# Scores of every chunk as plain float32 products instead of three float32r products of split q and k

## The chip, the core and the metric

The kernel runs on one core of a Trainium2 chip. The core has a matrix engine (TensorE, PE in the rows; its weight loads are PEld), a vector engine (VectorE, DVE), a scalar engine (ScalarE, ACT), a general engine (GpSimd, POOL) and a queue engine that starts transfers (SyncE, SP). Each engine works through its own list of instructions in order and waits where a semaphore says so. The metric is the device time of one execution in microseconds; several runs give a median.

## The reference

For two batches of 768 rows the reference computes an attention layer with 8 heads of 64 columns, then two feed-forward blocks. Cut to what matters here:

```python
scores = scale * np.matmul(q, k.transpose(0, 1, 3, 2))      # scale 1/8
keep = is_global | is_local                                 # first 8 keys, and the last 96
scores = np.where(keep, scores + bias, -1e9)
a = softmax(scores)
attn = np.matmul(a, v)                                      # to (2, 768, 512)
h = relu(attn @ w_in)
x = (h * sigmoid(conv3(h))) @ w_out
u, v = split(relu(x @ w_in2))
out = (u * (w_spatial @ norm(v) + b_spatial)) @ w_out2
```

Only the line with `scores` is computed in another way by the change; what is computed stays the same.

## The kernel before

The 2 x 768 rows are cut into six chunks of 256 rows (three for each batch). In a chunk there are four units, each a pair of heads, and in a unit two steps of 128 rows. So the attention has 24 units and 48 steps. A step goes through these tasks, in the order of the functions `scores`, `soften`, `halves`, `weigh` and `turn_x`:

- scores (L801): for both heads of the pair, q times 256 columns of k, into two PSUM banks. Head 0 lies in partitions 0 to 63 and head 1 in 64 to 127.
- soften: VectorE adds the bias and takes the extreme of each row (L820, tile `sb`, and `nm` beside it), for chunks 2 to 5 a fixed power is added to it (L833, tile `nb`, on GpSimd or VectorE), and ScalarE takes the exponential (L838).
- halves: for chunks 0 and 1 (`PLAINS`) TensorE turns the result (L851); for chunks 2 to 5 it is split into two float16 parts, `ph` (a cast, L474 on ScalarE or L478 on VectorE, and a subtraction, L488 on GpSimd or VectorE), which a transfer turns into `pt`.
- weigh: products with v (L906 plain, L912 to L914 in float16 parts), then VectorE divides (L918, L922, L923, tile `xk`).
- turn_x: TensorE turns `xk` (L954), and it is split into float16 parts `x`.

The same engines also do the first feed-forward block (L1028 products with w1, L1041 to L1066 the convolution and the gate, the parts `hh` and `hl`, L1098 products with w2) beside the attention, decode the float64 weights into float16 parts (L655 to L670 on ScalarE and VectorE, a cast, and a subtraction on GpSimd), and afterwards do the second block (L1173, L1246, L1278, L1308).

How the scores are made depends on the chunk. `NATS` lists the chunks whose q and k go into the products as they were loaded, and `qk_load` makes no parts of them. For the others ScalarE casts the whole tile of q and k (672 columns) to float32r (`qh`), and GpSimd or VectorE subtracts it from the tile, which leaves the low part in place (`qk` as float32r). The lines of `scores` that choose:

```python
if u // NPAIR in NATS:
    pairs = [(self.m("qk", u), self.m("qk", u))]
    cost, reads = 0.79, [("qk", u)]
else:
    hi, lo = self.m("qh", u, dt=F32R), self.m("qk", u, dt=F32R)
    pairs = [(hi, hi), (lo, hi), (hi, lo)]
    cost, reads = 0.57, [("qk", u), ("qh", u)]
```

The order on each engine isn't the order of the source. A planner (`Plan`) collects tasks with a cost for each engine that may do them, works out in six rounds which engine takes which task and when, and writes the instructions in that order; the lists are then fixed. A task's cost, the 0.79 and 0.57 above among them, so decides also where other tasks stand and on which of two engines a cast or subtraction runs. Until a planned time of 70 us the planner fills planned gaps of TensorE with products that nobody reads (L999).

Of the kernel before, what the change touches and what calls it, by code (L numbers as in the profile page):

```python
# [40 lines left out]

LEAD_TICKS, LEAD_STEPS = 12, 8

NATS, PLAINS = (0, 1, 2), (0, 1)

BIASES = 2

# [1535 lines left out]
```

## Time and profile before

| what | us |
|---|---|
| median of 3 runs | 381.29 (381.17 to 382.48) |
| the profiled execution, whole | 380.87 |
| its span, first to last instruction | 379.2 |
| TensorE busy | 360.5 |
| VectorE, ScalarE, GpSimd busy | 271.5, 265.4, 156.3 |

The span is what the engines' instructions cover; 1.67 us of the execution lie around it. TensorE's busy time overstates its work, since the ends of its pipelined products overlap: the distance from one start to the next is the better measure of what a product costs. The kernel has a first part to about 77 us, in which weights are decoded beside the attention of chunks 0 to 2; a middle part to about 245 us, with the attention of chunks 3 to 5 (scores from 90 to 187 us) and the rest of the first block; and a last part that is products almost alone.

### The profile page before, as it was taken

What the parts mean: (1) busy time and instruction counts of PE and PEld (TensorE: products, weight loads), DVE (VectorE), ACT (ScalarE), POOL (GpSimd) and SP (SyncE); (2) the same over time, 40 slices, a digit from 0 to 9 for tenths busy, and PEclk for the clock granted to TensorE, in tenths of its full rate; (3) what the DMA queues carried; (4) which work ended last, traced back from release to release, by engine and by line L of the source; (5) the groups of instructions that cost most, each with busy time, mean ns of one, the idle gap of its engine ahead of it and who ended that gap; (6) DMA issues with size and microseconds to landing.
All of it is one profiled execution on the core that took longest, in us unless ns stands there. A gap on an engine that the chain in (4) does not pass through costs nothing.

```text
span 379.2 us, 7892 instructions
## 1 busy us (share of the span) xinstructions
PE 360.5 (95%) x2893; PEld 254.7 (67%) x2893; DVE 271.5 (72%) x695; ACT 265.4 (70%) x650; POOL 156.3 (41%) x221
## 2 busy tenths in 40 slices
PE   8989889788999999999999999999999999999995
PEld 5767767557877888888779766676456565555543
DVE  5899999977985798799896498678568355151610
ACT  5977999678997798799898467676976434232332
POOL 5253447866486578578664034142125200000000
PEclk9987999989999999999999999999999999999999
DMA  7979422567639534974669000005510000202022
GB/s 223 406 253 309 166 94 73 111 186 176 171 95 267 108 83 94 204 186 119 83 99 346 1 2 0 2 2 159 169 62 0 0 2 0 86 0 85 0 85 91
DMA packets 46254, 43.60 MB, mean 115 GB/s; under 512 B 34816, under 2 KB 36608, under 8 KB 45696
## 3 DMA queue, kind: packets, MB, share of 16 engines
q1 hardware_dynamic: 46208, 43.03, 39.9%
q8 instruction: 24, 0.39, 0.4%
q14 instruction: 22, 0.18, 0.1%
HBM read 31.48 MB, written 3.15 MB: 91 GB/s over the span
## 4 chain that ended last, share of the span: by engine, by line
PE 51%; DVE 25%; ACT 11%; issue 6%; POOL 3%; DMA 2%; DVEq 0%; POOLq 0%; ACTq 0%
PE bank L1278 12%; PE bank L1308 8%; PE bank L1246 8%; PE bank L1098 6%; DVE wk_dt_float L665 5%; PE bank L1173 5%; DVE bank L1041 5%; DVE wk_dt_float L670 4%; DVE sb_dt_float L820 3%; PE bank L801 3%; PE bank L1028 3%; DVE wk_dt_float L662 3%; DMA pt_dt_float<-ph_dt_float 2%; ACT sb_dt_float L838 2%; PE bank L999 1%
## 5 line engine op out<-in xcount | busy, mean ns | idle before, releaser
L1028 PE MATMUL bank<-x_dt_float,w1h_dt_float 128*128 128x260 f16 (+1 forms) x384 | 65.1, 273 | 0.5 <-ACT pt_dt_float L474 0.4
L1098 PE MATMUL bank<-hl_dt_float,w2h_dt_float 128*128 128x254 f16 (+2 forms) x192 | 52.9, 275 | 1.4 <-POOL hl_dt_float L488 1.3
L1098 PE MATMUL bank<-hh_dt_float,w2l_dt_float 128*128 128x254 f16 (+2 forms) x192 | 52.9, 276 | 0.3 <-POOL w2l_dt_float L488 0.3
L1098 PE MATMUL bank<-hh_dt_float,w2h_dt_float 128*128 128x254 f16 (+2 forms) x192 | 53.0, 276 | 0.0
L1028 PE MATMUL bank<-x_dt_float,w1l_dt_float 128*128 128x260 f16 (+1 forms) x192 | 52.3, 273 | 0.0
L1041 DVE SCALAR_TENSOR_TENSOR bank<-hp_dt_float,cwt,bank 128x254 f32<-128x254 f32 (+2 forms) x96 | 46.0, 484 | 5.9 <-ACT bank L1035 3.4
L1278 PE MATMUL bank<-ws_dt_float,vn_dt_float 128*128 128x384 f16 x288 | 47.3, 326 | 0.0
L488 POOL TENSOR_TENSOR hl_dt_float<-ac_dt_float,hh_dt_float 128x256 f16<-128x256 f32 (+2 forms) x44 | 32.6, 747 | 33.5 <-ACT hh_dt_float L474 28.8
L488 POOL TENSOR_TENSOR ph_dt_float<-sb_dt_float,ph_dt_float 128x512 f16<-128x512 f32 x29 | 36.6, 1264 | 18.7 <-ACT ph_dt_float L474 16.7
L1028 PEld LDWEIGHTS <-w1h_dt_float 128*128 128x128 f16 x384 | 36.7, 97 | 7.3 <-issue 1.8
L1098 PEld LDWEIGHTS <-w2h_dt_float 128*128 128x128 f16 x384 | 36.8, 99 | 6.7 <-ACT sb_dt_float L838 0.3
L1278 PEld LDWEIGHTS <-vn_dt_float 128*128 128x128 f16 x288 | 28.2, 98 | 18.8
L820 DVE CUSTOM_DVE_ANT_0 sb_dt_float<-bank,bias_dt_float 128x256 f32<-128x256 f32 (+1 forms) x96 | 35.0, 400 | 5.4 <-PE bank L801 3.1
L838 ACT ACTIVATE sb_dt_float<-sb_dt_float,nb_dt_float 128x256 f32<-128x256 f32 (+1 forms) x64 | 30.0, 496 | 8.0 <-POOL nb_dt_float L833 5.6
L474 ACT CAST g_dt_float<-bank 128x384 f16<-128x384 f32 x16 | 7.7, 479 | 33.8 <-DVE bank L1285 33.8
L1246 PE MATMUL bank<-ys_dt_float,w3uh_dt_float 128*128 128x384 f16 x128 | 31.2, 326 | 0.0
L1282 DVE SCALAR_TENSOR_TENSOR bank<-bank,bb_dt_float 128x384 f32<-128x384 f32 x16 | 9.1, 566 | 29.4 <-PE bank L1278 29.4
L1308 PE MATMUL bank<-w4h_dt_float,g_dt_float 128*128 128x512 f16 (+1 forms) x104 | 28.9, 363 | 0.0
L1173 PE MATMUL bank<-w3vh_dt_float,ys_dt_float 128*128 128x512 f16 x96 | 28.5, 379 | 0.0
L1308 PEld LDWEIGHTS <-g_dt_float 128*128 128x128 f16 x156 | 15.2, 98 | 15.6
L665 DVE SCALAR_TENSOR_TENSOR wk_dt_float<-raw_dt_float,wk_dt_float 128x512 int32<-128x512 int32 x28 | 24.9, 896 | 0.2
L662 DVE TENSOR_SCALAR wk_dt_float<-wk_dt_float 128x512 int32<-128x512 int32 x28 | 18.6, 673 | 8.5 <-ACT wk_dt_float L655 8.4
(157 smaller groups left out, 890.8 us busy)
## 6 DMA issues: line engine op xcount, KB each, us to landing
raw_dt_float<-in_w SPq DMA_DIRECT2D x20, 512.0 KB, 5.1
qk_dt_float<-in_qk SPq DMA_DIRECT2D x24, 336.0 KB, 3.9
v_dt_float<-in_vb SPq DMA_DIRECT2D x4, 1024.0 KB, 6.0
out_x<-wk_dt_float SPq DMA_DIRECT2D x11, 256.0 KB, 2.0
raw_dt_float<-in_wst SPq DMA_DIRECT2D x6, 384.0 KB, 4.7
raw_dt_float<-in_w3v SPq DMA_DIRECT2D x4, 512.0 KB, 6.4
raw_dt_float<-in_w3u SPq DMA_DIRECT2D x4, 512.0 KB, 6.2
v_dt_float<-in_vb SPq DMA_DIRECT2D x2, 768.0 KB, 6.1
```

Source lines behind the costliest of these rows:

```text
L488: self.engines[e].tensor_tensor(out=out, in0=in0, in1=in1, op=ALU.subtract)
L662: nc.vector.tensor_scalar(out=fi, in0=fi, scalar1=3, scalar2=None, op0=ALU.logical_shift_left)
L665: nc.vector.scalar_tensor_tensor(out=fi, in0=lo, scalar=29, in1=fi, op0=ALU.logical_shift_right, op1=ALU.bitwise_or)
L820: nc.vector.tensor_tensor_reduce(out=sb[:, h, :n], in0=self.ps(self.sp[s][h])[:, :n], in1=self.m("bias", 2 * p + h)[:, t0 : t0 + n], scale ...
L838: nc.scalar.activation(out=sb[:, h, :n], in_=sb[:, h, :n], func=AF.Exp, scale=-1.0, bias=nb[:, h : h + 1])
L1028: nc.tensor.matmul(self.ps(acc)[:, :nx], w[f][:, k * P : (k + 1) * P], x[:, k, x0:], start=k == n == 0, stop=k == 3 and n == 2,)
L1041: nc.vector.scalar_tensor_tensor(out=ac(), in0=near(j), scalar=tap(j), in1=ac(), op0=ALU.mult, op1=ALU.add)
L1098: nc.tensor.matmul(ps(), w[2 * d + k // 4][:, k % 4 * P : (k % 4 + 1) * P], x, start=k == n == 0, stop=k == 7 and n == 2,)
L1173: nc.tensor.matmul(ps(), x[:, y, k, tk], w[k], start=n == 0, stop=n == 11)
L1246: nc.tensor.matmul(ps(), w[e4][:, k * P : (k + 1) * P], x[:, y, k, s], start=n == 0, stop=n == 11)
L1278: nc.tensor.matmul(ps(), v[:, k, x, ek], w[:, k, s], start=n == 0, stop=n == 17)
L1308: nc.tensor.matmul(ps(), x[:, y, k, tk], w[k][:, at], start=n == 0, stop=n == 11)
```

## The change

`NATS` now lists all six chunks:

```diff
-NATS, PLAINS = (0, 1, 2), (0, 1)
+NATS, PLAINS = (0, 1, 2, 3, 4, 5), (0, 1)
```

`PLAINS` is as before: chunks 2 to 5 keep the fixed power and the float16 parts of the probabilities. For the 12 units of chunks 3 to 5 the cast `qh` and the subtraction `qk` go, and each of their 24 steps has two float32 products (one for each head) in place of six float32r products. The planner gets other tasks and costs and so gives another order: the fill products L999 are 33 instead of 35; six `nb` additions go from VectorE to GpSimd, so do four `hl` subtractions and two `ph` subtractions, and two `ph` casts go from ScalarE to VectorE.

TensorE's list at the first step of chunk 3 (`qh` and `qk` are q and k of a unit, `xk` an attention result to be turned):

```order
-L801 MATMUL bank<-qh_dt_float32r 128x256 x2
-L801 MATMUL bank<-qh_dt_float32r,qk_dt_float32r 128x256 x2
-L801 MATMUL bank<-qk_dt_float32r,qh_dt_float32r 128x256 x2
+L801 MATMUL bank<-qk_dt_float_85 128x256 x2
```

Six products of a step are two.

VectorE's list around the division of the last unit of chunk 1 (L918 to L923; `xk` is what TensorE turns next, `wk` a weight that is being decoded, `ys` a part of the first block's result):

```order
 L665 SCALAR_TENSOR_TENSOR wk_dt_float_135<-raw_dt_float_134,wk_dt_float_135 128x512
-L670 SCALAR_TENSOR_TENSOR wk_dt_float_135<-raw_dt_float_134,wk_dt_float_135 128x512
 L484 SCALAR_TENSOR_TENSOR ys_0_dt_float_202<-bank,ys_0_dt_float_202 128x254
 L918 TENSOR_SCALAR r_dt_float_158<-bank 128x4
 L922 RECIPROCAL r_dt_float_158<-r_dt_float_158 128x4
 L923 TENSOR_TENSOR xk_dt_float_156<-bank,r_dt_float_158 128x256
+L670 SCALAR_TENSOR_TENSOR wk_dt_float_135<-raw_dt_float_134,wk_dt_float_135 128x512
```

The last step of a weight's decoding (L670) stood ahead of the division and stands behind it now.

VectorE's list some twenty instructions later, around the divisions of chunk 2's first two units:

```order
 L1041 SCALAR_TENSOR_TENSOR bank<-hp_dt_float_183,cwt,bank 128x256 x2
-L488 TENSOR_TENSOR ph_dt_float_203<-sb_dt_float_129,ph_dt_float_203 128x512
-L1066 SCALAR_TENSOR_TENSOR ac_dt_float_184<-bank,hp_dt_float_183 128x256
+L478 CAST ph_dt_float_203<-sb_dt_float_136 128x512
 L918 TENSOR_SCALAR r_dt_float_148<-bank 128x4
 L922 RECIPROCAL r_dt_float_148<-r_dt_float_148 128x4
 L923 TENSOR_TENSOR xk_dt_float_149<-bank,r_dt_float_148 128x256
```

A subtraction and a gate ahead of the division have gone, and a cast, which needs a later step's exponential, stands there now.

## Rows read from the trace of the kernel before

**Rows 1.** Page, part 1: busy us (share of the span) xinstructions.

```profile
PE 360.5 (95%) x2893; PEld 254.7 (67%) x2893; DVE 271.5 (72%) x695; ACT 265.4 (70%) x650; POOL 156.3 (41%) x221
```

**Rows 2.** Stretches: length, busy time of each engine (instructions), granted clock, DMA share, GB/s.

```profile
70.00:80.00 10.00, 6.63 (x42) 5.00 (x42) 9.26 (x21) 6.80 (x16) 7.96 (x10) 0.86 0.73 193
...
90.00:100.00 10.00, 8.72 (x104) 7.43 (x101) 9.65 (x28) 9.52 (x26) 4.88 (x9) 1.00 0.88 181
...
120.00:130.00 10.00, 10.00 (x106) 8.29 (x104) 5.68 (x20) 6.64 (x18) 4.44 (x7) 1.00 0.61 132
...
150.00:160.00 10.00, 10.00 (x118) 8.44 (x116) 7.59 (x24) 7.35 (x18) 7.05 (x10) 1.00 0.81 176
```

**Rows 3.** TensorE's waits from 85 to 245 us: total, times, longest.

```profile
PE bank L954 <- DVE xk_dt_float L923: 2.9, 3, 1.3
PE bank L1098 <- POOL hl_dt_float L488: 1.3, 2, 0.8
PE bank L912 <- DVE nm_dt_float L820: 0.5, 1, 0.5
PE bank L912 <- DMA pt_dt_float<-ph_dt_float: 0.2, 1, 0.2
```

**Rows 4.** TensorE in order of time, a float32 step: start, duration, operation.

```profile
82.49 0.70 PE L801 MATMUL bank<-qk_dt_float 64*128 64x256 f32 x4
83.12 0.28 PE L1098 MATMUL bank<-hh_dt_float,w2h_dt_float 128*128 128x254 f16 x1
```

**Rows 5.** TensorE in order of time, a float32r step and what follows it.

```profile
122.39 0.39 PE L801 MATMUL bank<-qh_dt_float32r 64*128 64x256 f32 x2
...
122.93 0.20 PE L912 MATMUL bank<-vh_dt_float,pt_dt_float 128*128 128x65 f16 x1
```

**Rows 6.** Groups by form: xcount, busy us, mean ns, idle before.

```profile
L474 ACT CAST qh_dt_float32r<-qk_dt_float 128x672 fp32r<-128x672 f32 x12 | 9.0, 753 | 0.2 <-PE bank L801 0.2
L488 POOL TENSOR_TENSOR qk_dt_float32r<-qk_dt_float,qh_dt_float32r 128x672 fp32r<-128x672 f32 x11 | 17.8, 1616 | 0.2
L488 DVE TENSOR_TENSOR qk_dt_float32r<-qk_dt_float,qh_dt_float32r 128x672 fp32r<-128x672 f32 x1 | 1.3, 1314 | 0.6 <-ACT qh_dt_float32r L474 0.6
L833 POOL TENSOR_TENSOR nb_dt_float<-nm_dt_float,shift 128x2 f32<-128x2 f32 x26 | 10.7, 413 | 4.0 <-DVE nm_dt_float L820 3.6
L478 DVE CAST vn_dt_float<-wk_dt_float 128x512 f16<-128x512 f32 x1 | 1.4, 1376 | 0.0
```

**Rows 7.** VectorE in order of time, 73 to 77 us.

```profile
74.40 1.68 DVE L670 SCALAR_TENSOR_TENSOR wk_dt_float<-raw_dt_float,wk_dt_float 128x512 int32<-128x512 int32 x1
76.00 0.41 DVE L484 SCALAR_TENSOR_TENSOR ys_dt_float<-bank,ys_dt_float 128x254 f16<-128x254 f32 x1
...
76.73 0.42 DVE L923 TENSOR_TENSOR xk_dt_float<-bank,r_dt_float 128x256 f32<-128x256 f32 x1
```

**Rows 8.** TensorE in order of time, 77 us; [idle before <-releaser].

```profile
77.21 0.69 PE L954 MATMUL bank<-ident,xk_dt_float 128*128 128x128 f32 x2 [3.37 <-DVE xk_dt_float L923]
```

**Rows 9.** Short stretches around the same wait, columns as in rows 2.

```profile
76.50:77.00 0.50, 0.00 (x0) 0.00 (x0) 0.45 (x2) 0.50 (x2) 0.19 (x1) 1.00 0.91 377
77.50:78.00 0.50, 0.50 (x4) 0.38 (x3) 0.33 (x2) 0.50 (x2) 0.50 (x2) 0.50 1.05 442
80.50:81.00 0.50, 0.50 (x4) 0.25 (x4) 0.11 (x1) 0.50 (x2) 0.00 (x0) 0.92 1.10 216
```

**Rows 10.** TensorE in order of time, waits from 90 to 117 us.

```profile
92.23 0.44 PE L954 MATMUL bank<-ident,xk_dt_float 128*128 128x128 f32 x2 [1.28 <-DVE xk_dt_float L923]
...
103.81 0.19 PE L912 MATMUL bank<-vh_dt_float,pt_dt_float 128*128 128x65 f16 x1 [0.48 <-DVE nm_dt_float L820]
...
112.11 0.27 PE L1098 MATMUL bank<-hl_dt_float,w2h_dt_float 128*128 128x256 f16 x1 [0.82 <-POOL hl_dt_float L488]
```

**Rows 11.** Chain of waits, ScalarE's pieces before that: start, us.

```profile
91.12 0.43 ACT sb_dt_float L838
91.88 0.52 ACT ph_dt_float L474
```

## The prediction

> **What bounds the kernel now.** First I read the page's busy times: TensorE 95%, VectorE 72%, ScalarE 70%, GpSimd 41% [rows 1]. The reader is to see that TensorE leads, but that a share over the whole run does not say where it waits. So next I read the stretches of 10 us [rows 2]. From 70 to 80 us TensorE is busy 6.63 of 10 us and VectorE 9.26: here VectorE, which decodes the weights, holds the end. From 90 to 100 us TensorE has 8.72 while VectorE and ScalarE have 9.65 and 9.52: TensorE is held up by engines that are nearly full. From 120 to 130 and from 150 to 160 us TensorE is busy throughout, and VectorE and ScalarE have 2.4 to 4.3 us of slack: TensorE alone is the bound. Third I read what TensorE waited for from 85 to 245 us, the part that the change touches directly [rows 3]: 2.9 us in three waits for an attention result `xk`, 1.3 us in two for `hl`, 0.5 and 0.2 us in two more before the products with v. That is 4.9 us in all, and it is the most that less work on the other engines can give back there. The helpers lose some 30 us of busy time below; almost none of it can show in the total.
>
> **The change part by part.**
>
> *Score products.* A float32 step starts at 82.49 us and the next product at 83.12: 0.63 us [rows 4]. A float32r step starts at 122.39 and the next product at 122.93: 0.54 us [rows 5]. So each of the 24 steps costs TensorE 0.09 us more, 24 x 0.09 = +2.2 us. Both rows are at the full granted clock and include the switch to what follows. I take all of it as being on the path, because TensorE has no slack in most of the stretches. If every step stood just ahead of a wait, it would cost nothing; so the term lies between 0 and +2.2.
>
> The Trainium skill ("FP8 and Floating Point Precision", section "TensorE Precision Notes") says that a true float32 product takes four passes through the array, and that the reduced form truncates float32 to what the array takes natively, which I read as one pass. By that rule alone a step would be 2 x 4 x 256 = 2048 columns against 6 x 256 = 1536, at 2.4 GHz an estimate of 0.85 against 0.64 us, and 24 steps would cost +5.1 us. The trace has less for both, 0.63 and 0.54 us; the two heads of a step use different halves of the array's rows, and their records overlap. Here the measured step decides.
>
> *Casts and subtractions that go.* ScalarE loses 12 casts of 0.753 us, 9.0 us. GpSimd loses 11 subtractions of 1.616 us, 17.8 us, and VectorE one of 1.3 us [rows 6]. None is on TensorE's path by itself: from 120 us on TensorE was busy beside all of them [rows 2]. What they may give is a part of the waits. Four of the 12 casts stand before 110 us, where ScalarE is full, so its list is some 3 us shorter when TensorE makes its waits of 1.28 us for `xk`, 0.48 us before the products with v and 0.82 us for `hl` [rows 10], 2.6 us. I take half, -1.3 us, since the float32r cast at 88 us is only one of many pieces that the chain runs through, and the exponential and cast at 91 to 92 us [rows 11] stay. Of the remaining 2.3 us (the other two waits for `xk`, the second for `hl` and the one for a transfer [rows 3]) I take a third, -0.8: TensorE is nearly full from there on, and what it waits for last is the end of the attention's own chain. Together -2.1, with ends 0 and -4.9. Six `nb` additions of 0.41 us and six more subtractions come to GpSimd, about 7 us against 17.8 that leave, so its list is shorter anyhow.
>
> *The division at 77 us.* This is no part of the edit itself; it comes from the new order. VectorE's L670 runs from 74.40 and the next instruction starts at 76.00; only then come `ys`, the division and `xk` at 76.73 [rows 7]. TensorE had been idle for 3.37 us when it turned `xk` at 77.21 [rows 8]. In the new order L670 stands behind the division, the rest of VectorE's list up to there has the same tasks in a slightly other order, and TensorE has the same products ahead of it. So `xk` is ready 1.6 us earlier: -1.6 us, ends 0 and -3.37. What is late instead is the decoded block of w2 that L670 finishes; its cast and subtraction follow up to 1.6 us later, and TensorE has two blocks of twelve products and two score steps of 0.63 us ahead of its use, which cover it.
>
> *The clock after it.* The granted clock is 1.00 in that wait, 0.50 from 77.5 to 78.0 and 0.92 from 80.5 to 81.0 [rows 9]: it fell to the 1.2 GHz level after TensorE had been idle for 3.37 us, and came back some 3.5 us later. At half speed 3.5 us do the work of 1.75. After the wait of 1.28 us at 92.23 [rows 10] the stretch of 90 to 100 us shows 1.00 throughout [rows 2]. The new wait of about 1.8 us lies between the two, nearer to the one that held, but the 10 us before it are also thinner. I take half, -0.85 us, ends 0 and -1.75.
>
> *Others.* Two fill products fewer, two casts moved to VectorE and single moves of casts behind 245 us I cost at nothing: VectorE has 2.4 to 4.3 us of slack in 10 where TensorE is full [rows 2], and TensorE's own work hides them. Where that cover is missing (80 to 100 us) they are a rival below.
>
> *Sum.* +2.2 - 2.1 - 1.6 - 0.85 = -2.35 us. The profiled execution took 380.87 us (span 379.2 and 1.67 around it), so 378.5 us. It lies 0.4 us below the median of 381.29; I leave the forecast at 378.5. The ends of all terms together would be 380.87 + 2.2 = 383.1 and, with the products at 2.2, 380.87 + 2.2 - 4.9 - 3.4 - 1.75 = 373.0.
>
> **The rivals.**
>
> *The waits stay (381.5 us).* The attention of a chunk is a long chain over all engines: scores, bias, exponential, split, a turn by transfer, products, division. If it is this chain's length and not the load of ScalarE that makes TensorE wait, nothing comes back of the 4.9 us, and the clock falls as before. Then it is +2.2 - 1.6: 381.5. For it: the waits for `xk` are waits for the last link of that chain, and one is for a transfer [rows 3]. Against: from 90 to 100 us ScalarE and VectorE are over 95% busy [rows 2], so the chain is queued and not only long.
>
> *A cast on VectorE holds the division (383.9 us, slower).* In the new order a `ph` cast stands right ahead of the division of chunk 2's first units. It needs an exponential from ScalarE, which ended at 91.55 in the trace, with the cast of the same kind following at 91.88 [rows 11], and VectorE can't pass it. If that exponential doesn't come earlier, VectorE casts from 91.6 (1.38 us by the one cast of that form on VectorE [rows 6]), divides in about 0.75 us, and TensorE turns `xk` at about 93.8 to 94.6 in place of 92.23, a loss of up to 2.4 us. Then 380.87 + 2.2 + 2.4 - 1.6 = 383.9. It decides if ScalarE reaches this exponential less than 2 us sooner than before. For it: one more link between two full engines. Against: a subtraction on VectorE and a gate stood in the same place before, and ScalarE has lost two float32r casts and two `ph` casts ahead of it, some 2.7 us.
>
> *Float32 products at the price of four passes (381.4 us).* If products beside other work, not the few steps at 82 us, show the real price, the sum has 2.9 us more: 378.5 + 2.9. This is the skill's rule above as a rival. Against: the step at 82.49 us stands between blocks of other products, as the new ones will, and has 0.63 us [rows 4].
>
> **How the numbers follow.** The forecast has 0.50, with a range of its own of 376.0 to 379.6: the clock wholly kept or lost (0.85 either way), the waits given back by half more or less. The waits stay has 0.27, the cast on VectorE 0.18, four passes 0.05. A measurement of this kernel tells about 0.5% (1.9 us) from no change, so faster is below 379.4 and slower above 383.2. Of the forecast's 0.50 some 0.46 lie below 379.4, and 0.05 of the second case (the clock held) with it: faster 0.51. Same is the rest of the forecast, most of the second case and all of the fourth: 0.31. Slower is 0.18, the third case. The range of 375.2 to 383.6 leaves out about 1 in 10 above and less below.
>
> **What the new profile would show.** Score steps of 0.63 us from start to the next product, 24 more of them; no `qh` cast. TensorE's wait for `xk` at 75 to 77 us is 1.5 to 2.2 us in place of 3.37, and the clock after it is 1.00 where the half-speed term is right, or 0.50 where it is not. TensorE's waits from 85 us to the end of the first block sum to about 2.8 us in place of 4.9. From 250 us on the two traces run alike with a constant shift. I am wrong if TensorE's waits in that part are as long as before or longer, above all if VectorE stands waiting for ScalarE ahead of L478; if steps cost over 0.7 us; or if the wait at 77 us is still over 3 us because VectorE gets there later.

## The result, and the profile after

The changed kernel takes 385.50 us (385.29 to 385.67, median of 4 executions) against 381.23 for the kernel before in the same comparison, a ratio of 1.0106 with a 95% interval of 1.0086 to 1.0126. Timed again later it gave 1.0125 (1.0106 to 1.0144). So it is slower by 4 to 5 us where 2.4 us less were forecast, and it lies above the range. The profiled execution has a span of 383.6 us, 4.4 more than before.

Part 1 of the page after, with the columns of [rows 1]:

```profile
PE 363.7 (95%) x2843; PEld 252.7 (66%) x2843; DVE 265.4 (69%) x685; ACT 258.0 (67%) x636; POOL 143.7 (37%) x221
```

Every engine that was to be relieved is relieved: VectorE 6.1 us, ScalarE 7.4, GpSimd 12.6. Only TensorE has 3.2 us more. That is not all work: in the stretch of 70 to 80 us below it is busy for 10.00 us in place of 6.63, at a granted clock of 0.68 in place of 0.86.

The product steps are as forecast. TensorE in order of time at a step of chunk 4, to be read as [rows 4, 5]:

```profile
120.87 0.70 PE L801 MATMUL bank<-qk_dt_float 64*128 64x256 f32 x4
...
121.51 0.20 PE L912 MATMUL bank<-vh_dt_float,pt_dt_float 128*128 128x65 f16 x1
```

That is 0.64 us to the next product, where the float32r step had 0.54. Next the stretches, as in [rows 2], with three more:

```profile
70.00:80.00 10.00, 10.00 (x60) 7.63 (x60) 9.13 (x26) 6.83 (x17) 7.36 (x11) 0.68 0.77 207
...
90.00:100.00 10.00, 8.25 (x90) 6.25 (x88) 9.54 (x30) 8.62 (x23) 5.68 (x8) 1.00 0.86 225
...
120.00:130.00 10.00, 10.00 (x101) 7.41 (x99) 6.45 (x22) 7.01 (x19) 3.50 (x7) 1.00 0.57 118
...
140.00:150.00 10.00, 9.38 (x97) 7.27 (x95) 7.17 (x21) 7.67 (x17) 6.84 (x13) 1.00 0.61 147
150.00:160.00 10.00, 10.00 (x110) 7.88 (x108) 6.66 (x20) 5.49 (x14) 3.35 (x5) 1.00 0.69 156
...
170.00:180.00 10.00, 8.84 (x90) 6.63 (x87) 9.79 (x30) 9.60 (x27) 7.53 (x14) 1.00 0.48 118
180.00:190.00 10.00, 9.10 (x89) 6.72 (x88) 9.79 (x21) 6.91 (x17) 6.50 (x7) 1.00 0.38 73
```

The reader is to see that TensorE now has gaps from 140 to 150 and from 170 to 190 us (9.38, 8.84 and 9.10, where it had 9.93, 10.00 and 9.12), with VectorE at 9.79 of 10 in the last two. The waits of TensorE from 85 to 245 us, against [rows 3]:

```profile
PE bank L1098 <- POOL hl_dt_float L488: 2.7, 4, 1.3
PE bank L1028 <- DVE ac_dt_float L1066: 1.1, 1, 1.1
PE bank L801 <- DVE nm_dt_float L820: 0.9, 1, 0.9
PE bank L954 <- DVE xk_dt_float L923: 0.8, 2, 0.6
PE bank L954 <- DVE ac_dt_float L1066: 0.4, 1, 0.4
PE bank L1098 <- POOL hp_dt_float L1050: 0.2, 1, 0.2
PE bank L912 <- DVE ac_dt_float L1066: 0.2, 1, 0.2
```

The waits for `xk` fell from 2.9 to 0.8 us, as hoped; but all waits together grew from 4.9 to 6.3 us where 2.8 were forecast, and their releasers are others. Where they stand, from TensorE's list in order of time (a wait is in the brackets):

```profile
144.81 0.27 PE L1098 MATMUL bank<-hl_dt_float,w2h_dt_float 128*128 128x258 f16 x1 [0.47 <-POOL hl_dt_float L488]
...
178.06 0.27 PE L1098 MATMUL bank<-hl_dt_float,w2h_dt_float 128*128 128x254 f16 x1 [0.38 <-POOL hl_dt_float L488]
...
179.13 0.27 PE L1098 MATMUL bank<-hl_dt_float,w2h_dt_float 128*128 128x254 f16 x1 [0.59 <-POOL hl_dt_float L488]
...
189.36 0.70 PE L801 MATMUL bank<-qk_dt_float 64*128 64x256 f32 x2 [0.90 <-DVE nm_dt_float L820]
...
200.38 0.44 PE L954 MATMUL bank<-ident,xk_dt_float 128*128 128x128 f32 x2 [0.56 <-DVE xk_dt_float L923]
```

Setting the start of the same product of TensorE in the two traces side by side tells when the time went. The changed kernel is 1.55 us ahead at 84 us, 1.1 ahead at 140, even at 160, and 2.8 us behind from 207 us on; a wait for `hl` at 240 us that only the kernel before has leaves 2.15 us at the last product. So it falls back by 3.7 us from 84 us on: some 2 us of it are the dearer steps, and the rest is the growth of the waits.

The other 2.2 us arise behind the last product. The rows of L1579, the block that ends the program, show TensorE's part of it (PEldq is the sequencer that issues its weight loads; count, durations in ns, first and last start: at the first one TensorE has reached the block); before:

```profile
L1579 PEldq DRAIN  x2: 8/8/8, 377.3 to 378.6; - x2
```

and after:

```profile
L1579 PEldq DRAIN  x2: 8/8/8, 382.8 to 383.2; - x2
```

The last copy of ScalarE starts right behind the last product; before:

```profile
375.01 0.38 ACT L472 ACTIVATE wk_dt_float<-bank 128x256 f32<-128x256 f32 x1 [0.93 <-PE bank L1308]
```

and after:

```profile
377.15 0.38 ACT L472 ACTIVATE wk_dt_float<-bank 128x256 f32<-128x256 f32 x1 [0.93 <-PE bank L1308]
```

From there TensorE needed 2.3 us to reach its end block before, and 5.7 us after. Nothing that the change touches stands there.

### The profile page after: what moved, and what is told of

Same layout as the page of the kernel before. It is cut to its first block, busy times and chain, and to the rows that moved or that the text cites. A ratio compares the mean times of both kernels' runs of the same rounds, so it can differ in the third digit from the quotient of the medians.

```text
span 383.6 us, 7742 instructions
## 1 busy us (share of the span) xinstructions
PE 363.7 (95%) x2843; PEld 252.7 (66%) x2843; DVE 265.4 (69%) x685; ACT 258.0 (67%) x636; POOL 143.7 (37%) x221
## 4 chain that ended last, share of the span: by engine, by line
PE 45%; DVE 6%; ACT 4%; issue 2%; POOL 1%; ACTq 0%; POOLq 0%
PE bank L1278 12%; PE bank L1308 8%; PE bank L1246 8%; PE bank L1173 8%; PE bank L1098 5%; PE bank L1028 3%; DVE bank L1041 2%; DVE wk_dt_float L665 1%; ACT sb_dt_float L838 1%; ACT junk_dt_float L501 1%; DVE sb_dt_float L820 1%; DVE wk_dt_float L662 1%; DVE wk_dt_float L670 1%; ACT bank L1035 1%; DVE ac_dt_float L1066 0%
## 5 line engine op out<-in xcount | busy, mean ns | idle before, releaser
L488 POOL TENSOR_TENSOR hl_dt_float<-ac_dt_float,hh_dt_float 128x254 f16<-128x254 f32 (+2 forms) x48 | 36.5, 772 | 32.8 <-ACT hh_dt_float L474 29.8
L488 POOL TENSOR_TENSOR ph_dt_float<-sb_dt_float,ph_dt_float 128x512 f16<-128x512 f32 x31 | 39.2, 1268 | 20.2 <-ACT ph_dt_float L474 11.4
L801 PE MATMUL bank<-qk_dt_float 64*128 64x256 f32 x192 | 35.8, 451 | 1.1 <-DVE nm_dt_float L820 0.9
L670 DVE SCALAR_TENSOR_TENSOR wk_dt_float<-raw_dt_float,wk_dt_float 128x512 int32<-128x512 int32 x28 | 24.9, 894 | 0.2
```

Of the source, the lines that this page charges most:

```text
L488: self.engines[e].tensor_tensor(out=out, in0=in0, in1=in1, op=ALU.subtract)
L670: nc.vector.scalar_tensor_tensor(out=fi, in0=hi, scalar=-(2**31), in1=fi, op0=ALU.bitwise_and, op1=ALU.bitwise_or)
L801: nc.tensor.matmul(self.ps(sp[h])[:, :256], x[r, t * P : (t + 1) * P], y[r, k0 : k0 + 256], start=n == 0, stop=n == len(pairs) - 1,)
```

## The experiments

All ratios are to the kernel before, timed on the same chip beside the runs. The first four take the change apart.

**Products alone.** Casts and subtractions stay (the low part is written over `qh`), the products of chunks 3 to 5 are float32; 24 products in the branch that is never taken (`dense`) keep TensorE's end block in its place. The edit of `scores`:

```diff
-            pairs = [(hi, hi), (lo, hi), (hi, lo)]
+            pairs = [(self.m("qk", u), self.m("qk", u))]
```

> The kernel before with the casts and subtractions of chunks 3 to 5 kept (their results are not read by the products any more), and the 24 score steps as float32 products: the price of the products alone. Price by the steps in the traces, 24 x 0.08 to 0.09: 383.2 us. Hidden in waits: 381.2. Four passes for float32 against three products of one pass: 386.3.

Measured: 382.15 us, ratio 1.0003 (0.9986 to 1.0021), or -0.5 to +0.8 us. In its trace TensorE is 1.5 us later at the last product, but 1.1 us of that are there at 84 us, ahead of the first new step. Its waits from 85 to 245 us are 3.8 in place of 4.9 us: a large part of the +2.2 us goes into time that TensorE had waited. The +5.1 us of the rival with four passes are out.

**Old order, casts gone.** The same products and the same 24 unexecuted ones, and the casts and subtractions emit nothing, though the planner still reckons with them; so everything else keeps its place. The edit of `qk_load`, its first lines shortened:

```diff
-        self.parts(CH + KW, self.m("qh", u, dt=F32R), ...)
+        none = lambda e: None
+        add(copy_cost(n), none, reads=[("qk", u)], writes=[("qh", u)])
+        add(sub_cost(n), none, reads=[("qk", u), ("qh", u)], writes=[("qk", u)])
```

> The order of the kernel before, with the 12 casts and 12 subtractions of chunks 3 to 5 left out and their 24 score steps as float32 products; the planner still reckons with the tasks that are gone, so that nothing else moves, and TensorE's program keeps its end in place. Theory A (the new order brings the waits): float32 products +2.0 us, a part of the waits given back, 381 to 382.5 us. Theory B (float32 products at these places are what costs, whatever the order): 383.3 us, the changed kernel without its 2.2 us at the end. Theory C (my prediction's terms without the division moved): 380.87 + 2.2 - 2.1 = 381.0.

Measured: 380.35 us, ratio 0.9965 (0.9950 to 0.9980). This is the work of the changed kernel in the order of the one before, and it is faster than both. TensorE waits 2.4 us from 85 to 245 us, near the 2.8 of my forecast. Against the run with the products alone (1.0003) the casts and subtractions that go give 0.4%, 1.4 us. A second run of the same order, further down, agrees (0.9970).

**The changed kernel with its end block in place.** 25 products (100 TensorE instructions) in the branch that is never taken.

```diff
-        self.widen()
+        self.widen(); [self.nc.tensor.matmul(...) for _ in range(25)]
```

> The changed kernel with 25 float32 products (100 TensorE instructions) put into the branch that is never taken, so that TensorE's last instructions lie at the same place in its program as in the kernel before; nothing that is executed changes. Theory A (of the loss of 4.3 us, 2.2 us arise after the last product, because the block at the end now has to be fetched): 383.3 us, and from the last product to the end of the span 4.3 us in place of 6.5. Theory B (the tail is the effect of what ScalarE, VectorE and the transfers do at the end): 385.5 us and 6.5 us.

Measured: 384.61 us (383.68 to 386.79), ratio 1.0087 (1.0055 to 1.0119). TensorE reaches its end block at 380.4 us, 2.3 us behind ScalarE's last copy at 378.07:

```profile
L1579 PEldq DRAIN  x2: 8/8/8, 380.4 to 382.4; - x2
```

So the place of the end block makes the late end in the trace, and from the end of the last product to the end of the span it is 1.7 us less (4.85 against 6.53). By the ratios the total gains 0.7 us against the first timing of the changed kernel (1.0106) and 1.4 us against the second (1.0125), and the intervals overlap. The greater part of the loss is elsewhere: the same work takes 4.3 us more in the new order than in the old one (384.61 against 380.35).

**The kernel before with its end block moved**, by 156 instructions in the same branch.

```diff
-        self.widen()
+        self.widen(); [self.nc.tensor.matmul(...) for _ in range(39)]
```

> The kernel before with 39 float32 products (156 instructions) in the branch that is never taken, so that TensorE's last instructions lie against the fetched pieces of its program as in the changed kernel. Theory A (fetch at the end): 383.4 us against 381.2, the added 2.2 us all after the last product. Theory B (no such effect): 381.2 us.

Measured: 382.65 us, ratio 1.0023 (1.0009 to 1.0037): slower by 0.9 us, not 2.2, and not where I said. The span is as before; the time around it, about 1.8 us before, is 2.2 to 3.7 us in these executions. So 156 instructions that aren't executed cost something, but neither the size nor the place is the one that I expected.

**The old order without the 24 products** in that branch (end block 96 instructions earlier).

```diff
-        self.widen(); [self.nc.tensor.matmul(...) for _ in range(24)]
+        self.widen()
```

> The kernel with the old order and float32 products (380.35 us), without the products in the branch that is never taken: TensorE's end block lies 96 instructions earlier in its program, near the place that it has in the changed kernel (100 earlier). Theory A (the end block has to be fetched there): 381.5 to 382.6 us, with TensorE's last block starting over 4 us after its last product in place of 2.3. Theory B: 380.35 us, no change.

Measured: 380.62 us, ratio 0.9970 (0.9954 to 0.9986): no change. In this order an earlier end block costs nothing.

**The changed kernel again**, with no edit.

> The changed kernel once more, to weigh its end. If the 2.2 us behind the last product are there in every execution: ratio 1.0106 as in the first run, and 5.7 us from the last product to TensorE's last block. If the first profile showed a rare case: 384.6 us, as with the end block moved, and 2.4 us.

Measured: 386.47 us, ratio 1.0125. The last copy starts at 378.99, the end block is reached at 384.8:

```profile
L1579 PEldq DRAIN  x2: 8/8/8, 384.8 to 385.1; - x2
```

From ScalarE's last copy to the block it is 5.7 and 5.8 us in the two profiles of the changed kernel, and 2.2 to 2.9 us in the traces of all other kernels here.

**What in the plan makes the order bad?** Two things differ for the planner: tasks that are gone, and 0.79 in place of 0.57 us for a step. Each was tried alone, and a third price, all with float32 products and no casts executed:

```diff
-            cost, reads = 0.57, [("qk", u), ("qh", u)]
+            cost, reads = 0.79, [("qk", u), ("qh", u)]
```

> Float32 products for chunks 3 to 5, no casts and subtractions executed, as in the run with the old order (380.35 us); but the planner now reckons a score step of these chunks at 0.79 us, as in the changed kernel, and still with the tasks that are gone. TensorE's end block stays in place. Theory A (the price of 0.79 us, against the measured 0.63, is what makes the order bad): close to the changed kernel with its end block in place, 383.5 to 385. Theory B (the tasks missing in the plan make it bad): 380.0 to 381.

Measured: 383.80 us, ratio 1.0062 (1.0039 to 1.0085).

```diff
-            cost, reads = 0.79, [("qk", u)]
+            cost, reads = 0.79 if u < 12 else 0.57, [("qk", u)]
```

> The changed kernel, its planner without casts and subtractions, but with the steps of chunks 3 to 5 reckoned at 0.57 us as before; end block in place. Theory A (the price makes the order bad): 380 to 381.5. Theory B (the missing tasks make it bad): 383.5 to 385. If any change of the plan gives an order that is off by some us at random, it lies anywhere between, and both of these runs tell only that.

Measured: 387.60 us, ratio 1.0152 (1.0101 to 1.0203). Its executions fall into two groups, three from 384.52 to 385.66 us and three from 389.54 to 390.54, so the size of this ratio is unclear; the lower group alone is about 0.9% above the kernel before.

```diff
-            cost, reads = 0.79, [("qk", u)]
+            cost, reads = 0.79 if u < 12 else 0.64, [("qk", u)]
```

> The changed kernel, with the steps of chunks 3 to 5 planned at 0.64 us, about what they take in the trace, in place of 0.79; end block in place. If it is the wrong price that makes the order bad: 380 to 381.5. If any new plan is worse than the one that these costs were fitted to, as the plans at 0.57 (387.6) and with the old tasks at 0.79 (383.8) suggest: 383 to 387.

Measured: 385.04 us, ratio 1.0095 (1.0068 to 1.0122). So neither the price nor the missing tasks make the loss alone: each of the four new plans is slower, by 0.6 to 1.0% where the size is clear, the one with the measured price among them.

**Where in the program?** Two orders put together from the two plans: one up to a planned time of 125 us, the other behind it, with the same work; PSUM banks are given anew behind the seam.

```diff
-        order = self.order()
+        order = hybrid(self, "new", 125.0)
```

> Same work as the changed kernel (float32 products, no casts and subtractions), in an order put together from two: up to a planned time of 125 us the order of the changed kernel, behind it the order of the kernel before. In the traces the new order gains about 1 us up to 135 us and loses 4.4 us between 135 and 207 us, both against the old order with the same work (380.35 us). Theory A (the loss is made by the order behind 135 us): 379.0 to 380.4 us, faster than all kernels so far. Theory B (the new order has left work undone before 125 us, which is then late): 383 to 385.

Measured: 380.45 us, ratio 0.9983 (0.9964 to 1.0003).

```diff
-        order = self.order()
+        order = hybrid(self, "old", 125.0)
```

> The converse: the order of the kernel before up to a planned time of 125 us, the changed kernel's behind it, same work. Theory A (the order behind 135 us makes the loss): 380.35 + 4.4, 384 to 385.5. Theory B (the loss is laid up before 125 us): 380 to 381.

Measured: 385.24 us, ratio 1.0097 (1.0081 to 1.0113). The pair settles the place: the new order is harmless up to 125 us and costs all of the loss, 1.3% or some 5 us against the old order throughout, behind it.

The traces say the same. I take the product that TensorE starts at 125 us in the trace before, and the time from it to TensorE's last product. Against the kernel before that time is 3.6 us longer in each of the three profiles of the new order (the changed kernel twice, and with its end block in place), and 4.2 us longer with the new order behind 125 us alone; in the two profiles of the old order with the same work it is 0.8 and 0.7 us shorter, and 0.7 us shorter with the old order behind 125 us alone. By this measure the plan with the old tasks at 0.79 us loses nothing there (0.2 us shorter), so its loss lies ahead of it; the three plans without the tasks lose 3.6 us, 1.7 us (at 0.64) and 4.2 us (at 0.57). So the loss at this place, though not the total, goes with the missing tasks rather than the price; all but the first of these plans have one profile each.

TensorE's busy time from 130 to 210 us (sum of eight stretches, then the other engines) in the changed kernel:

```profile
sum 80.00, PE 76.44 PEld 61.08 DVE 65.91 ACT 65.46 POOL 43.25; mean PE 9.55 PEld 7.63 DVE 8.24 ACT 8.18 POOL 5.41
```

and in the old order with the same work:

```profile
sum 80.00, PE 79.53 PEld 64.86 DVE 67.72 ACT 69.26 POOL 43.88; mean PE 9.94 PEld 8.11 DVE 8.46 ACT 8.66 POOL 5.48
```

TensorE loses 3.1 of 80 us there though no other engine is busier. Its waits from 135 to 245 us with the old order:

```profile
PE bank L1098 <- POOL hl_dt_float L488: 0.5, 1, 0.5
PE bank L954 <- DVE xk_dt_float L923: 0.5, 1, 0.5
```

and with the new order behind 125 us:

```profile
PE bank L1098 <- POOL hl_dt_float L488: 1.8, 3, 0.8
PE bank L801 <- DVE nm_dt_float L820: 0.9, 1, 0.9
PE bank L954 <- DVE xk_dt_float L923: 0.6, 1, 0.6
PE bank L1098 <- POOL hp_dt_float L1050: 0.2, 1, 0.2
PE bank L912 <- DVE ac_dt_float L1066: 0.2, 1, 0.2
```

The lists differ by 2.7 us, the runs by 5. A stop costs more than its row says: two products of a block start 0.11 us apart though the record of each lasts 0.27 us, and a wait is counted only from the end of the record. From start to start, TensorE makes ten stops of over 0.33 us between 122 and 245 us with the new order, 7.0 us in all, and two with the old one, 1.5 us in all. That is most of the loss, in many small stops before products of several kinds.

**Which tasks?** First the changed kernel's order with the six `nb` and four `hl` back on VectorE (a line where tasks are emitted; `mine` are the ten):

```diff
-            self.tasks[i][1](e)
+            self.tasks[i][1]("DVE" if i in mine else e)
```

> The changed kernel with its end block in place (384.6 us) and its order, but the six nb additions and the four hl subtractions that stood on VectorE before run there again. Theory A (GpSimd, which got them, delivers hl and nb late, and TensorE's 2.7 us of waits for hl come from it): 382 to 383.2, waits for hl at most 1.3 us. Theory B (VectorE and ScalarE are late as well, the order of all of them is bad): 384 to 385, other waits in place of those for hl.

Measured: 383.82 us, ratio 1.0059 (1.0037 to 1.0081), about 1.1 us better than with the end block alone in place (1.0087; the intervals overlap). TensorE's waits for `hl` stay, one of 1.3 us now behind VectorE; behind 125 us it loses 2.9 us in place of 3.6.

Then the new order in which only the tasks `late` (decoding of w3, range reductions) go back to the neighbours `moved` that they had in the old one (`back` is empty in this run):

```diff
+        if x[0] not in late:
+            seq += [(i, e, x[2]) for i, e, _ in moved.get(x[0], [])]
+            seq.append((x[0], "DVE", x[2]) if x[0] in back else x)
```

> The changed kernel's order (384.6 us with the end block in place), in which only the decoding of four blocks of w3 (wk, w3vh, w3vl) and six reductions that look at ranges (L501, four of them over ys) stand again next to the tasks next to which they stood in the kernel before; the plan had put the last reductions and casts 6 to 11 us earlier, between the exponentials and the gates of chunk 5. Theory A (these tasks, which nothing waits for yet, hold up ScalarE and VectorE between 158 and 204 us and with them hl, ac and xk): 381.5 to 383.2 us, TensorE's waits between 140 and 207 us at least 1.5 us shorter. Theory B (the choice of GpSimd for hl and nb makes the loss): 384 to 385.

Measured: 385.14 us, ratio 1.0088 (1.0067 to 1.0110). This theory falls: the early decoding stands on the chain that ended last in the changed kernel's trace, and taking it away from there gains nothing (TensorE loses 4.0 us behind 125 us).

And both edits in one kernel; with "both", `back` holds the ten tasks:

```diff
-        order = hybrid(self, "late", 125.0)
+        order = hybrid(self, "both", 125.0)
```

> The same, and the six nb and four hl that stood on VectorE before are back there (alone that gave 383.82 us). If both hold TensorE up, each at another place: 380.3 to 382 us, close to the old order (380.35). If they are two sides of the same queue: no better than the better one alone, about 383. If the order of the gates and divisions themselves makes the loss: 383.5 to 385.

Measured: 384.31 us, ratio 1.0064 (1.0045 to 1.0082), no better than the ten tasks alone. Together with the run before: no single group of tasks that I picked is the cause.

**Whose list?** Behind 125 us TensorE's list from one plan, the lists of the other engines from the other one (for the converse run `first_pe` is `new`).

```diff
+    first_pe = "old"
+    lists = {}
+    for i, e, start in old:
+        if i not in done and (e == "PE") == (first_pe == "old"):
+            lists.setdefault(e, []).append((i, e, start))
+    for i, e, start in new:
+        if i not in done and (e == "PE") == (first_pe == "new"):
+            lists.setdefault(e, []).append((i, e, start))
```

> Work of the changed kernel; up to a planned time of 125 us the order of the kernel before on all engines; behind it TensorE's list from the kernel before and the lists of VectorE, ScalarE, GpSimd and SyncE from the changed kernel. With all lists old it was 380.35 us, with all new behind 125 us 385.24. Theory C (TensorE's own list makes the loss: it comes to products whose inputs are not ready): 380 to 381.5. Theory D (the lists of the other engines make it): 384 to 386. If lists of two plans do not fit each other, both this and its converse are 385 or more.

Measured: 386.14 us, ratio 1.0131 (1.0104 to 1.0157). TensorE's waits from 135 us on:

```profile
PE bank L954 <- DVE xk_dt_float L923: 2.3, 3, 1.2
PE bank L801 <- DVE nm_dt_float L820: 2.0, 1, 2.0
PE bank L912 <- DVE ac_dt_float L1066: 0.2, 1, 0.2
```

> The converse: behind 125 us TensorE's list from the changed kernel, all other lists from the kernel before. Theory C: 384 to 386. Theory D: 380 to 381.5. TensorE's two lists differ in five places there: a block of six w2 products, two blocks of twelve to twenty-four, two score steps and one turn stand elsewhere.

Measured: 383.52 us, ratio 1.0060 (1.0040 to 1.0081), with these waits:

```profile
PE bank L912 <- DMA pt_dt_float<-ph_dt_float: 1.3, 1, 1.3
PE bank L1098 <- DVE hl_dt_float L488: 0.9, 1, 0.9
PE bank L1098 <- POOL hl_dt_float L488: 0.7, 2, 0.5
PE bank L1098 <- POOL hp_dt_float L1050: 0.6, 1, 0.6
```

Both are bad. The new lists of the other engines are enough for the whole loss under TensorE's old list, where `xk` and `nm` come later; and TensorE's new list loses 1% against the old order under the old lists of the others, where it comes to w2 products and products with v whose inputs are not ready. But lists of two plans may lose time just because they don't belong together, and no run here tells that from a fault of either list. So the loss isn't divided between them.

## Why the prediction was wrong, step by step

- **Score products, +2.2.** A step costs what was forecast (0.64 and 0.54 us). That I took all of it as being on the path was wrong: alone it measures +0.1 us (-0.5 to +0.8), at the other of the two bounds that were stated. The rival of four passes is refuted by these two numbers. By the Trainium skill ("FP8 and Floating Point Precision", "TensorE Precision Notes"), which gives true float32 four passes, a step was estimated at 0.85 us; the trace of the changed kernel does not agree, with 0.64.
- **Casts and subtractions that go, -2.1.** Measured -1.4 us in the old order, TensorE's waits 2.4 against 2.8 us forecast. The mechanism holds there, with two thirds of the size, and the rival that the waits stay falls. The two terms together gave -1.3 us (0.9965), against +0.1 in my sum: in the old order the edit is better than forecast.
- **The division at 77 us, -1.6, and the clock behind it, -0.85.** The division came as forecast, at 74.95 in place of 76.73 us, and in the first profile TensorE turned `xk` without a wait:

```profile
74.95 0.42 DVE L923 TENSOR_TENSOR xk_dt_float<-bank,r_dt_float 128x256 f32<-128x256 f32 x1
...
76.58 0.44 PE L954 MATMUL bank<-ident,xk_dt_float 128*128 128x128 f32 x2
```

  But a wait that I had not looked for stood 7 us earlier, 1.78 us in place of 0.36, and the clock fell behind that one to 0.50, the 1.2 GHz level:

```profile
69.46 1.84 PE L906 MATMUL bank<-v_dt_float,pt_dt_float 128*128 128x65 f32 x8 [1.78 <-DVE nm_dt_float L820]
```

```profile
70.00:71.00 1.00, 1.00 (x7) 1.00 (x7) 1.00 (x3) 0.61 (x2) 0.41 (x1) 0.50 1.26 209
...
75.00:76.00 1.00, 1.00 (x5) 0.58 (x5) 1.00 (x2) 0.00 (x0) 1.00 (x2) 0.50 1.05 442
```

  So TensorE came late to `xk` because it ran at half speed. The second profile of the same kernel (`a1_changed_again`) has the same early wait, the clock held behind it, and the rest came as forecast: a wait of 2.04 us for `xk`, and the clock fell behind that one:

```profile
69.67 2.00 PE L906 MATMUL bank<-v_dt_float,pt_dt_float 128*128 128x65 f32 x16 [1.78 <-DVE nm_dt_float L820]
...
75.64 0.68 PE L954 MATMUL bank<-ident,xk_dt_float 128*128 128x128 f32 x2 [2.04 <-DVE xk_dt_float L923]
```

```profile
70.00:71.00 1.00, 1.00 (x11) 1.00 (x10) 1.00 (x3) 0.40 (x1) 0.58 (x1) 1.00 1.15 197
...
76.00:77.00 1.00, 1.00 (x7) 0.69 (x6) 1.00 (x1) 0.00 (x0) 0.63 (x1) 0.50 0.00 0
```

  So the clock term gave nothing back: it is at 0.50 for about 3.4 us before and in the second profile, and for nearly 7 us in the first. TensorE was 2.2 and 1.5 us ahead at 81 us all the same, but this did not last: at 125 us the two profiles are 1.4 us ahead and 0.4 us behind, and the new order up to 125 us with the old one behind it is no faster than the old order throughout (0.9983 and 0.9965).
- **The rival of a cast on VectorE** is refuted as a mechanism. VectorE did wait for the exponential, but the cast took 0.43 us and not the 1.38 of [rows 6], and TensorE waited for `xk` by 0.29 us. The row of 1.38 us was no price for this place, since GpSimd worked beside it (last section).

```profile
88.81 0.43 DVE L478 CAST ph_dt_float<-sb_dt_float 128x512 f16<-128x512 f32 x1 [0.57 <-ACT sb_dt_float L838]
```

```profile
90.77 0.44 PE L954 MATMUL bank<-ident,xk_dt_float 128*128 128x128 f32 x2 [0.29 <-DVE xk_dt_float L923]
```

- **The step that failed is "Others", costed at nothing** because "VectorE has 2.4 to 4.3 us of slack in 10 where TensorE is full". The sum has no other term for where the new order puts the tasks behind 95 us, and that order costs some 5 us behind 125 us (0.9965 to 1.0097). The reason did not hold in the trace before either: it was read from two stretches, and in two others TensorE is just as full with 0.3 and 0.4 us of VectorE left:

```profile
160.00:170.00 10.00, 10.00 (x109) 8.40 (x108) 9.72 (x31) 9.59 (x28) 6.63 (x11) 1.00 0.71 168
170.00:180.00 10.00, 10.00 (x110) 8.26 (x108) 9.59 (x31) 9.46 (x27) 8.22 (x15) 1.00 0.45 136
```

  And slack in a stretch of the old order does not say when an input is ready in another order. What the runs show in its place are the many small stops of TensorE, with waits of 6.3 us where 2.8 were forecast. One rival let the waits stay as they were, and one looked at a single place ahead of 95 us; none let them grow behind it.
- **"From 250 us on the two traces run alike with a constant shift"** held up to the last product (2.15 us throughout) and failed behind it, where 2.2 us more arose in the trace; putting the end block back in place gains 0.7 to 1.4 us of the total, within overlapping intervals.

Settled are the place of the loss (behind a planned 125 us) and that it is the order and not the work. Open is why each new plan came out worse: prices, missing tasks, ten tasks on GpSimd and early decoding were each tried and none explains it alone; whether the loss lies in TensorE's list or in those of the others is not divided. Open too is what TensorE's end block waits for; that it is its instructions being fetched is only argued, from the effect of code that isn't executed.

## What to carry to other kernels

Where a planner writes the order, take a change apart into the work and the order: keep the removed tasks in the plan as empty ones and time that first. Here it turned a kernel slower by 1% into one faster by 0.35% (0.9965, 0.9950 to 0.9980). Slack read from the old order is no cover for a new one; a forecast for a new order needs a range as wide as what other orders of the same work give, here 0.35% faster to 1% slower, and perhaps 1.5% in one plan. Slack is read from every stretch in which the engine is full, not from two.

## What the runs showed of the hardware that was not expected

- TensorE reached its end block 5.7 and 5.8 us behind the start of ScalarE's last copy in the two profiles of the changed kernel, and 2.3 us behind it once 100 instructions that are never executed stood in front. With 156 such instructions the kernel before took 0.9 us longer, outside the span.
- One float32 product in place of three float32r products is nearly free here: 0.64 in place of 0.54 us a step, and 24 such steps gave 1.0003.
- A float16 cast of 128x512 on VectorE took 1.38 us in the trace before and 0.41 to 0.45 us in three places of the one after. The slow one ran beside a subtraction of GpSimd, the second in the row below, and ended 0.3 us behind it; the fast ones had no subtraction of GpSimd beside them. That the one holds up the other would fit, and no run here tests it.

```profile
250.97 2.64 POOL L488 TENSOR_TENSOR vn_dt_float<-wk_dt_float,vn_dt_float 128x512 f16<-128x512 f32 x2 [9.97 <-ACT vn_dt_float L474]
...
252.52 1.38 DVE L478 CAST vn_dt_float<-wk_dt_float 128x512 f16<-128x512 f32 x1
```

- The clock after the same wait of 1.78 us at 69 us fell in one profile of the changed kernel and held in the other.
